# Batch 0's short rows first, the combining product in high and low halves, and new planning numbers

## The chip, the cores and the metric

The kernel runs on one core of one Trainium2 chip. The metric is device microseconds of one execution, the median of several runs. TensorE (PE) multiplies into PSUM; VectorE (DVE), ScalarE (ACT) and GpSimd (POOL) do the elementwise work; SyncE (SP) issues most of the loads and stores.

## The reference

Four batches of channel attention, whose result goes straight into a gated convolution. Cut to what is computed, with B = 4, N = 6336 rows, C = 256 channels, K = 5 taps:

```python
qn = q / (norm(q, axis=1) + 1e-06);  kn = k / (norm(k, axis=1) + 1e-06)
a = softmax(kn.transpose(0, 2, 1) @ qn / tau)        # 256 x 256 for each batch
x = v @ a
gate = sigmoid(sum(conv_w[j] * xp[:, j:j + S, :] for j in range(K)))  # xp: x with 4 zero rows ahead
out = (gate * (x @ w_val)) @ w_out
```

The three weights (`w_val`, `conv_w`, `w_out`) arrive as float64; q, k and v as float32.

## The kernel before, in words

**Scores.** N is 49 times 128 rows and 64 more, the *short rows* (`RP` = 49, `REST` = 64). For each batch the products k^T q are summed over the rows in one PSUM bank, `s_ps`. Row sets of 128 are loaded in groups of three (`GROUP`), the first group of a batch holding one. A row set is multiplied either whole in fp32 (`raw`; two products, one for each half of the channels) or split: ACT casts it to a high half `hi` (fp32r), POOL makes the low half `lo`, and PE does hi·hi, lo·hi and hi·lo, six products of 256 columns. In batch 0 two or three row sets of each group are done whole, in the first groups of batch 1 two. `group_tasks` (line 387 on) makes these tasks: `L` the load (line 402), `C` and `O` the halves, `S` the square on ACT (line 453) and `A` its addition to `acc_ps` on DVE or to `acc` on POOL (line 457), `P` the products (line 485). In batches 1 to 3 the short rows come with the first group, behind its full row set; in batch 0 they are a group of their own, put in at place 9 (`REST_AT`). Before the first data are there, PE multiplies zeros: eleven products (`idle(11)`), and four more after the first row set (`idle(4)`).

**Softmax.** Once a batch's rows are summed, `softmax_tasks` runs a chain over all engines: the sums of squares are joined (line 545), `norms` brings them onto the partitions by PE (line 535), then root, inverse, scale, exponentials (line 579), their sum, and the division (line 591) to the attention `a`. It is cast to halves (line 595 high, POOL low), which are the weights of the *mixing product* x = v·a. Further on, PE transposes `a` (line 604), ACT copies the transpose from PSUM to `at` (line 608), and the *combining product* `combine` multiplies it with w_val (line 614): four fp32 products of 256 columns, which give a·w_val, the weights of the *value product* v·(a·w_val). Its halves are made by `high_w` on ACT (line 618) and `low_w` on DVE (line 621).

**Output steps.** Thirteen steps of up to 508 positions for each batch, 52 in all. v comes in transposed (line 682) and is split (lines 686, 689). A step has two mixing products `X`, one for each half of the channels (six fp32r products each, into one of two buffers of `x_ps`), the first tap by ACT (`G`, line 720), the other taps by DVE (`D`, line 723: eight in a step), the sigmoid, two value products `U` (into `val_ps`), their multiplication with the gate on DVE (`B`, line 741), the split of the result (lines 747, 750), four output products with w_out (`F`, line 769), copies by ACT (line 778) and the store. The output products of a step stand behind the value products of the next one in PE's order.

**PSUM.** `s_ps` and `acc_ps` have a bank each, `x_ps` two, and the other four banks (tag `bank`) are shared by `val_ps`, `o_ps` (norms, transposes, combining and output products) and `w_ps` (below).

**Weights.** The float64 words are turned into float32 on DVE in ten or eleven steps of one instruction (`prepare_weights`, lines 317 to 349), spread among its other work; `WORDS` is 2 here. w_out ends as a high and a low half (`wo_hi`, `wo_lo`), w_val as one fp32 array in `wa`.

**What sets the order.** Two things. `line` (lines 861 to 909) is PE's order, written as a loop: the row groups are spread over the output steps, at such a pace that the last of them falls into step `LAST_ROWS` = 52 - 13 - `LATE`, and behind a batch's last group come its `norms`, `transpose` and `combine`, each some places apart (`SPREAD`). Steps behind LAST_ROWS give the last tap of their second half to ACT and POOL (`shared`, line 806), and every other one of those two or more further on puts `x_ps` in the banks of `s_ps` and `acc_ps` (`late`). The class `Plan` then walks through all tasks with a cost for each (`deadlines`, `run`): on each engine it takes the one that is due first by `line`, by the chain behind it, and by `WANTED` (latest wanted times for the weights). The order so found is what each engine runs; `NARROW`, `REACH` and the costs written in each `task` call feed it. So a change of one number can move instructions on all engines.

## Time and profile before

| | |
|---|---|
| median of the runs | 595.4 us (three runs, 595.34 to 595.72) |
| the profiled execution | 594.63 us |
| its span | 592.8 us |
| TensorE clock granted | 1.00 |
| DMA, mean over the span | 179 GB/s |
| score products, line 485, lo·hi and hi·lo | 306 each, 285 and 283 ns |
| mixing and value products, line 697 | 416 each, 385 and 380 ns |

The span runs from the first to the last instruction that the profiler records; the execution's own time is 1.8 us longer, and is what the runs measure. PE's matmuls are pipelined, so the mean time of one matmul is longer than the distance from its start to the next one's; where the text compares costs on PE it uses distances between starts. A matmul in unsplit fp32 leaves two records in the profile, one in fp32r leaves one. Views name a tile by its program's name and an instruction by the line that issued it.

### The profile page before, as it was taken

How to read it: one execution, taken by the hardware profiler on the slowest of the kernel's cores; microseconds unless marked ns; L12 is line 12 of the kernel's file. 1: busy time of each engine (PE TensorE's matmuls, PEld its weight loads, DVE VectorE, ACT ScalarE, POOL GpSimd, SP SyncE). 2: the span in 40 equal slices, each digit the busy share in tenths (PEclk: the TensorE clock that was granted, in tenths of full speed). 3: DMA queues.
4: the chain of work that ended last, by engine and by line, in shares of the span. 5: the costliest groups of instructions: out<-in, count | busy, mean ns of one | idle time of the engine just before them, and what ended most of it. 6: DMA issues, size and time to landing. Idle time of an engine off the chain costs nothing.

```text
span 592.8 us, 10519 instructions
## 1 busy us (share of the span) xinstructions
PE 587.0 (99%) x3647; PEld 531.8 (90%) x3647; DVE 507.5 (86%) x783; ACT 476.6 (80%) x580; POOL 511.7 (86%) x247
## 2 busy tenths in 40 slices
PE   9999999999999999999999999999999999999997
PEld 8998888989989989989988898998998898888887
DVE  3998899999998989969879898978978988888784
ACT  6787998889899878778789987878767877777754
POOL 5996999999989999999997999999993868777843
PEclk9999999999999999999999999999999999999999
DMA  8999959775659978779555897869845265554214
GB/s 343 367 379 293 256 125 196 186 188 132 173 142 217 209 181 208 143 202 223 146 153 155 209 205 201 163 145 237 157 111 118 73 142 133 133 142 121 70 41 123
DMA packets 154944, 105.83 MB, mean 179 GB/s; under 512 B 111115, under 2 KB 137995, under 8 KB 154891
## 3 DMA queue, kind: packets, MB, share of 16 engines
q1 hardware_dynamic: 154467, 104.51, 69.8%
q8 instruction: 29, 0.48, 0.3%
q10 hardware_dynamic: 423, 0.65, 0.3%
q14 instruction: 25, 0.20, 0.1%
HBM read 79.18 MB, written 25.95 MB: 177 GB/s over the span
## 4 chain that ended last, share of the span: by engine, by line
PE 93%; ACT 3%; DVE 2%; issue 1%; POOL 0%; ACTq 0%; DVEq 0%; POOLq 0%
PE s_ps L485 25%; PE o_ps L769 22%; PE x_ps L697 22%; PE val_ps L697 22%; DVE gate L723 1%; PE o_ps L614 1%; ACT hi L426 0%; ACT sq L453 0%; ACT gate L734 0%; ACT o_sb L778 0%; DVE o_ps L564 0%; PE o_ps L535 0%; ACT gate L720 0%; PE x_ps L769 0%; ACT L553 0%
## 5 line engine op out<-in xcount | busy, mean ns | idle before, releaser
L723 DVE SCALAR_TENSOR_TENSOR gate<-x_ps,wa,gate 128x508 f32<-128x508 f32 (+1 forms) x401 | 267.6, 716 | 22.9 <-ACT gate L720 21.1
L429 POOL TENSOR_TENSOR lo<-raw,hi 128x1536 fp32r<-128x1536 f32 (+2 forms) x65 | 182.4, 2811 | 12.1 <-ACT hi L426 10.7
L689 POOL TENSOR_TENSOR v_lo<-v_raw,v_hi 128x1024 fp32r<-128x1024 f32 (+1 forms) x52 | 123.4, 2375 | 12.5 <-ACT v_hi L686 12.5
L750 POOL TENSOR_TENSOR g_lo<-gate,g_hi 128x1016 fp32r<-128x1016 f32 (+2 forms) x52 | 120.4, 2316 | 15.9 <-ACT g_hi L747 15.7
L457 DVE TENSOR_TENSOR acc_ps<-acc_ps,sq 128x512 f32<-128x512 f32 (+1 forms) x139 | 96.4, 694 | 33.8 <-ACT sq L453 30.5
L697 PE MATMUL x_ps<-v_hi,w 128*128 128x512 f32 (+2 forms) x416 | 110.2, 385 | 0.3 <-DVE gate L723 0.3
L697 PE MATMUL val_ps<-v_hi,w 128*128 128x508 f32 (+1 forms) x416 | 107.6, 380 | 0.0
L453 ACT ACTIVATE sq<-raw 128x1536 f32<-128x1536 f32 (+2 forms) x68 | 96.1, 1415 | 4.6 <-DMA raw<-in_k_dram 2.1
L426 ACT CAST hi<-raw 128x1536 fp32r<-128x1536 f32 (+2 forms) x65 | 77.8, 1204 | 15.8 <-DMA raw<-in_k_dram 11.9
L697 PEld LDWEIGHTS val_ps<-v_hi,w 128*128 128x128 f32 x416 | 75.9, 188 | 14.8
L778 ACT COPY o_sb<-o_ps 127x512 f32<-127x512 f32 (+1 forms) x99 | 57.5, 587 | 35.5 <-PE o_ps L769 35.3
L697 PEld LDWEIGHTS x_ps<-v_hi,w 128*128 128x128 f32 x416 | 73.2, 188 | 13.6 <-PE o_ps L769 0.5
L769 PE MATMUL o_ps<-wo_hi,g_hi 128*127 128x256 f32 (+1 forms) x396 | 80.0, 283 | 0.6 <-ACT o_sb L778 0.6
L769 PE MATMUL o_ps<-wo_lo,g_hi 128*127 128x256 f32 (+1 forms) x396 | 78.9, 281 | 0.0
L457 POOL TENSOR_TENSOR acc<-acc,sq 128x512 f32<-128x512 f32 (+1 forms) x53 | 68.8, 1298 | 9.7 <-ACT acc L448 6.4
L485 PE MATMUL s_ps<-lo,hi 128*128 128x256 f32 x306 | 76.7, 285 | 0.0
L485 PE MATMUL s_ps<-hi,lo 128*128 128x256 f32 x306 | 76.1, 283 | 0.0
L720 ACT ACTIVATE gate<-x_ps,wa 128x508 f32<-128x508 f32 (+1 forms) x104 | 67.4, 663 | 5.9 <-PE x_ps L697 5.4
L741 DVE TENSOR_TENSOR gate<-val_ps,gate 128x508 f32<-128x508 f32 (+1 forms) x104 | 66.7, 653 | 5.8 <-PE val_ps L697 3.0
L686 ACT CAST v_hi<-v_raw 128x1024 fp32r<-128x1024 f32 (+1 forms) x52 | 57.6, 1108 | 16.2 <-PE val_ps L697 12.9
L769 PEld LDWEIGHTS o_ps<-wo_hi,g_hi 128*127 128x127 f32 (+1 forms) x396 | 62.9, 187 | 3.9 <-ACT o_sb L778 0.8
L747 ACT CAST g_hi<-gate 128x1016 fp32r<-128x1016 f32 (+3 forms) x54 | 53.0, 981 | 16.2 <-DVE gate L741 15.5
(89 smaller groups left out, 946.3 us busy)
## 6 DMA issues: line engine op xcount, KB each, us to landing
raw<-in_q_dram SPq DMA_DIRECT2D x64, 384.0 KB, 5.9
v_raw<-in_v_dram SPq DMA_DIRECT2D x192, 128.0 KB, 6.1
raw<-in_k_dram SPq DMA_DIRECT2D x63, 384.0 KB, 6.6
out_dram<-o_sb SPq DMA_DIRECT2D x47, 448.0 KB, 3.2
out_dram<-o_sb SPq DMA_DIRECT2D x47, 60.0 KB, 3.0
v_raw<-in_v_dram SPq DMA_DIRECT2D x16, 64.0 KB, 2.4
out_dram<-o_sb SPq DMA_DIRECT2D x3, 240.0 KB, 2.6
raw<-in_q_dram SPq DMA_DIRECT2D x4, 128.0 KB, 3.1
```

Of the source, the lines that this page charges most:

```text
L426: nc.scalar.copy(t["hi"][r, js], t["raw"][r, js, :, :])
L429: nc.gpsimd.tensor_tensor(t["lo"][r, js], t["raw"][r, js, :, :], t["hi"][r, js].bitcast(F32), ALU.subtract)
L453: nc.scalar.activation(t["sq"][0:np_, ja:jb], t["raw"][0:np_, ja:jb], AF.Square)
L457: eng.tensor_tensor(st[key][0:np_], st[key][0:np_], t["sq"][0:np_, j], ALU.add)
L485: nc.tensor.matmul(st["s"][:, h, :], lhs, rhs, start="open" not in st, stop=stop)
L689: nc.gpsimd.tensor_tensor(t["vl"][:, :, 0:g, :], t["v"], t["vh"][:, :, 0:g, :].bitcast(F32), ALU.subtract)
L697: nc.tensor.matmul(dst, weights[b][:, which, ws, ch, hs], vs[:, ch, at + lo:at + hi_], start=n_ == 0, stop=n_ == len(ops) - 1)
L720: nc.scalar.activation(t["gate"][:, h, 0:w], t["x", h][:, 0:w], AF.Copy, scale=cw[:, h, 0:1])
L723: nc.vector.scalar_tensor_tensor(t["gate"][:, h, 0:w], t["x", h][:, k_:k_ + w], cw[:, h, k_:k_ + 1], t["gate"][:, h, 0:w], ALU.mult, ALU.add)
L741: nc.vector.tensor_tensor(t["gate"][:, h, 0:w], t["val", h][:, 0:w], t["gate"][:, h, 0:w], ALU.mult)
L750: eng.tensor_tensor(t["gl"][:, hs, 0:w], t["gate"][:, hs, 0:w], t["gh"][:, hs, 0:w].bitcast(F32), ALU.subtract)
L769: nc.tensor.matmul(t["o", p][0:rows, u * C:(u + 1) * C], gs[:, h, j * rows:(j + 1) * rows], ws[:, h, :], start=(u, n_) == (0, 0) if HEADS ...
```

## The change

Four things are done.

**Short rows.** In every batch the short rows now belong to the first group, and in batch 0 they stand ahead of its one full row set, in the loads, on PE, and in the squares. Batch 0's group of its own is gone, as is `REST_AT`. The zeros are nine at first, and none after the first row set.

**Combining product.** w_val is kept as two fp32r halves, `wv_hi` and `wv_lo`, as w_out was. Its preparation on DVE has one step less (the halves are not added), and ACT casts the high half (`high_weights`, line 356). The transposed attention is kept as halves too: ACT's copy rounds to `at_hi`, and a new DVE task `low_at` (line 610) makes `at_lo`. `combine` then has twelve fp32r products (hi·hi for all four blocks, then at_hi·wv_lo, then at_lo·wv_hi) in place of four fp32 ones.

**Planning numbers.** `SPREAD` has an entry for each batch, `LATE` is 5 (LAST_ROWS 34, not 35), `NARROW` is a set of batches with the same one in it, `REACH` and four times in `WANTED` differ, and the costs of the changed tasks are new.

**Order.** With these the plan comes out anew on all engines; of the 192 additions of squares DVE does 144 and POOL 48, where it was 139 and 53. PE's last 607 products are the same as before.

```diff
-START, HOP, DRAIN, SLOT, FLIGHT, REACH, RATE = 3.7, 0.12, 0.22, 0.45, 4.5, 1.5, 340000.0
+START, HOP, DRAIN, SLOT, FLIGHT, REACH, RATE = 3.7, 0.12, 0.22, 0.45, 4.5, 1.6, 340000.0
...
-NARROW, LATE = 1, 4
-SPREAD = ((0, 2, 2), (0, 1, 1, 1))
-REST_AT = 9
+NARROW, LATE = (0,), 5
+SPREAD = ((0, 0, 0, 0), (1, 2, 1), (1, 2, 2), (0, 1, 1))
 TABLE = 1.28
-WANTED = {("load", "conv"): 30, ("load", "val"): 17, ("load", "out"): 40, ("ready", "val"): 40, ("ready", "conv"): 36, ("ready", "out"): 60}
+WANTED = {("load", "conv"): 26, ("load", "val"): 17, ("load", "out"): 36, ("ready", "val"): 40, ("ready", "conv"): 34, ("ready", "out"): 66}
...
-    groups = {b: [(j, n, bool(b and REST and not j)) for j, n in rows_] for b in range(B)}
-    if REST:
-        groups[0].insert(REST_AT, (0, 0, True))
+    groups = {b: [(j, n, REST > 0 and not j) for j, n in rows_] for b in range(B)}
...
-    wv_sb = wa[:, 0:NW].rearrange("p (h e) -> p h e", h=NH)
...
+    halves_w = {part: [const.tile([P, NH, C], F32R, name=f"w{part[0]}_{side}") for side in ("hi", "lo")] for part in ("val", "out")}
+    (wv_hi, wv_lo), (wo_hi, wo_lo) = halves_w["val"], halves_w["out"]
...
-            if part != "out":
+            if part == "conv":
                 yield
                 nc.vector.tensor_tensor(w, w, fs, ALU.add)
...
+    def high_weights(part):
+        if WORDS == 2:
+            nc.scalar.copy(flat(halves_w[part][0]), w_high[part])
+
+    PREP = {"val": 10, "conv": 11, "out": 10}
...
-        parts = [(P, 0, n)] * (n > 0) + [(REST, n, 1)] * rest
+        parts = [(P, 0, n)] + [(REST, n, 1)] * rest
+        if b == 0:
+            parts.reverse()
...
+            for np_, j, nj in parts:
+                for s, src in ((0, q), (1, k)):
+                    rows = src[b, 0:RP * P].rearrange("(p j) c -> p j c", j=RP)[:, j0_:j0_ + n, :] if np_ == P else src[b, RP * P:N].unsqueeze(1)
+                    (nc.scalar if apart and s else nc.sync).dma_start(out=raw[0:np_, s, j:j + nj, :], in_=rows)
...
-                idle(11)
+                idle(9)
...
-            if (b, g, j) == (0, 0, 0):
-                idle(4)
...
-            nc.scalar.copy(t["at"].rearrange("p h c -> p (h c)"), t["at_ps"])
+            t["at"] = [soft_p.tile([P, NH, C], F32R, name=f"at_{side}") for side in ("hi", "lo")]
+            nc.scalar.copy(flat(t["at"][0]), t["at_ps"])
+
+        def low_at():
+            nc.vector.tensor_tensor(flat(t["at"][1]), t["at_ps"], flat(t["at"][0]).bitcast(F32), ALU.subtract)
 
         def combine():
             t["aw"] = ps.tile([P, 512], F32, name="o_ps", tag="bank")
-            for h in range(NH):
-                for h2 in range(NH):
-                    nc.tensor.matmul(t["aw"][:, h * C:(h + 1) * C], t["at"][:, h2, h * P:(h + 1) * P], wv_sb[:, h2, :],
-                                     start=h2 == 0, stop=h2 == NH - 1)
+            ops = [(x, y, h, h2) for x, y in ((0, 0), (0, 1), (1, 0)) for h in range(NH) for h2 in range(NH)]
+            for x, y, h, h2 in ops:
+                nc.tensor.matmul(t["aw"][:, h * C:(h + 1) * C], t["at"][x][:, h2, h * P:(h + 1) * P], halves_w["val"][y][:, h2, :],
+                                 start=(x, y, h, h2) == ops[0], stop=(x, y, h, h2) == ops[-1])
...
-        task(k_("combine"), "PE", 1.65, combine, deps=[k_("copy_at"), ("ready", "val"), ("prep", "val", PREP["val"] - 1 if WORDS == 2 else 0)], uses=[aw_i], takes=[aw_i])
+        task(k_("low_at"), "DVE", 0.6, low_at, deps=[k_("copy_at")], uses=[at_i])
+        task(k_("combine"), "PE", 1.4, combine, deps=[k_("copy_at"), k_("low_at"), ("ready", "val")], uses=[aw_i], takes=[aw_i], lead={k_("low_at"): 0.9})
...
-            for key, wait in zip(names, SPREAD[b < NARROW] if b else (0,) * 4):
+            for key, wait in zip(names, SPREAD[b]):
```

Rows of the queues, in the order in which each engine runs them, show where the instructions went; a row has the line, the operation, the written tile and the ones read, its size, and how often it repeats. PE's first products, before:

```order
L485 MATMUL s_ps<-zeros 128x256 x11
L485 MATMUL s_ps<-raw 128x256 x2
L485 MATMUL s_ps<-zeros 128x256 x4
L485 MATMUL s_ps<-raw 128x256 x16
L485 MATMUL s_ps<-hi 128x256 x2
```

and of the change:

```order
L486 MATMUL s_ps<-zeros 128x256 x9
L486 MATMUL s_ps<-raw 128x256 x20
L486 MATMUL s_ps<-hi 128x256 x2
L486 MATMUL s_ps<-lo,hi 128x256
L486 MATMUL s_ps<-hi,lo 128x256
```

The first two of the twenty whole products are the short rows', the next two the first full row set's; six products of zeros are gone.

PE at the first output step: the last score products ahead of it, value products `val_ps` of step 0 and mixing products `x_ps` of step 1. Before:

```order
L485 MATMUL s_ps<-lo,hi 128x256
L485 MATMUL s_ps<-hi,lo 128x256
L697 MATMUL val_ps<-v_hi,w 128x508 x4
L697 MATMUL val_ps<-v_lo,w 128x508 x2
L697 MATMUL x_ps<-v_hi,w 128x512 x4
L697 MATMUL x_ps<-v_lo,w 128x512 x2
L697 MATMUL x_ps<-v_hi,w 128x512 x4
L697 MATMUL x_ps<-v_lo,w 128x512 x2
L697 MATMUL val_ps<-v_hi,w 128x508 x4
L697 MATMUL val_ps<-v_lo,w 128x508 x2
```

and of the change:

```order
L486 MATMUL s_ps<-lo,hi 128x256
L486 MATMUL s_ps<-hi,lo 128x256
L486 MATMUL s_ps<-hi 128x256 x8
L700 MATMUL x_ps<-v_hi,w 128x512 x4
L700 MATMUL x_ps<-v_lo,w 128x512 x2
L700 MATMUL x_ps<-v_hi,w 128x512 x4
L700 MATMUL x_ps<-v_lo,w 128x512 x2
L700 MATMUL val_ps<-v_hi,w 128x508 x4
L700 MATMUL val_ps<-v_lo,w 128x508 x2
L700 MATMUL val_ps<-v_hi,w 128x508 x4
L700 MATMUL val_ps<-v_lo,w 128x508 x2
```

The first value product of step 0 stood ahead of the mixing products of step 1; now both value products stand behind them, and eight score products of high halves ahead.

ACT at batch 0's combining product, from the copy of the transposed attention to the first taps of step 0 (`gate`). Before:

```order
L608 COPY at<-o_ps 128x512
L595 CAST w<-a 128x512
L376 CAST wo_hi<-w_ps 128x512
L686 CAST v_hi<-v_raw 128x1024
L426 CAST hi<-raw 128x512
L618 CAST w<-o_ps 128x512
L720 ACTIVATE gate<-x_ps,wa 128x508 x2
```

and of the change:

```order
L607 CAST at_hi<-o_ps 128x512
L594 CAST w<-a 128x512
L356 CAST wo_hi<-w_ps 128x512
L454 ACTIVATE sq<-raw 128x1536
L689 CAST v_hi<-v_raw 128x1024
L427 CAST hi<-raw 128x512
L723 ACTIVATE gate<-x_ps,wa 128x508
L620 CAST w<-o_ps 128x512
L723 ACTIVATE gate<-x_ps,wa 128x508
```

A square of three row sets has come in behind the cast of w_out, and the high half of the combined weights (`w<-o_ps`) stands between the two first taps.

More of the change, by code (lines that the diff above doesn't have):

```diff
@@ L286 @@
     NW = NH * C
-    wa = const.tile([P, NW + NH * K], F32, name="wa")
-    wb = const.tile([P, NW], F32, name="wb")
-    wv_sb = wa[:, 0:NW].rearrange("p (h e) -> p h e", h=NH)
-    cw = wa[:, NW:].rearrange("p (h k) -> p h k", h=NH)
-    wo_hi = const.tile([P, NH, C], F32R, name="wo_hi")
-    wo_lo = const.tile([P, NH, C], F32R, name="wo_lo")
-    parts_w = {"val": wa[:, 0:NW], "conv": wa[:, NW:], "out": wb}
+    w_conv = const.tile([P, NH * K], F32, name="wa")
+    cw = w_conv.rearrange("p (h k) -> p h k", h=NH)
+    halves_w = {part: [const.tile([P, NH, C], F32R, name=f"w{part[0]}_{side}") for side in ("hi", "lo")] for part in ("val", "out")}
+    (wv_hi, wv_lo), (wo_hi, wo_lo) = halves_w["val"], halves_w["out"]
+    flat = lambda w: w.rearrange("p h e -> p (h e)")
+    parts_w = {"conv": w_conv}
+    for part in ("val", "out"):
+        parts_w[part] = flat(halves_w[part][1]) if WORDS == 2 else const.tile([P, NW], F32, name=f"w{part[0]}_sb")
     w_raw, w_high = {}, {}
@@ L339, in prepare_weights @@
             yield
-            low = wo_lo.rearrange("p h e -> p (h e)") if part == "out" else w
-            nc.vector.scalar_tensor_tensor(low, lo, 2.0 ** -35, fs, ALU.mult, ALU.mult)
+            nc.vector.scalar_tensor_tensor(w, lo, 2.0 ** -35, fs, ALU.mult, ALU.mult)
             yield
@@ L348, in prepare_weights @@
             w_high[part] = fs
-            if part != "out":
+            if part == "conv":
                 yield
                 nc.vector.tensor_tensor(w, w, fs, ALU.add)
-        elif part == "out":
-            nc.vector.tensor_copy(wo_hi, wb.rearrange("p (h e) -> p h e", h=NH))
-            nc.vector.tensor_tensor(wo_lo, wb.rearrange("p (h e) -> p h e", h=NH), wo_hi.bitcast(F32), ALU.subtract)
-    PREP = {"val": 11, "conv": 11, "out": 10}
+        elif part != "conv":
+            hi, low = map(flat, halves_w[part])
+            nc.vector.tensor_copy(hi, w)
+            nc.vector.tensor_tensor(low, w, hi.bitcast(F32), ALU.subtract)
+    def high_weights(part):
+        if WORDS == 2:
+            nc.scalar.copy(flat(halves_w[part][0]), w_high[part])
+    PREP = {"val": 10, "conv": 11, "out": 10}
     def weight_tasks():
@@ L373, in weight_tasks @@
                      uses=[holds[part], ("bank", "w", part)], takes=[("bank", "w", part)] if k == 0 else [])
-            task(("ready", part), "DVE" if part == "conv" else "ACT" if part == "out" else None, 0.5 if part == "out" else 0.07,
-                 {"val": lambda: None, "conv": lambda: nc.vector.reciprocal(rtau, tau_sb),
-                  "out": lambda: WORDS == 2 and nc.scalar.copy(wo_hi.rearrange("p h e -> p (h e)"), w_high["out"])}[part],
+            task(("ready", part), "DVE" if part == "conv" else "ACT", 0.07 if part == "conv" else 0.5,
+                 (lambda: nc.vector.reciprocal(rtau, tau_sb)) if part == "conv" else lambda part=part: high_weights(part),
                  deps=[("prep", part, n - 1)], uses=[holds[part], ("bank", "w", part)])
@@ L402, in load @@
             raw = raw_p.tile([P, 2, GROUP, C], F32, name="raw")
-            for s, src in ((0, q), (1, k)):
-                if n:
-                    main = src[b, 0:RP * P].rearrange("(p j) c -> p j c", j=RP)
-                    (nc.scalar if apart and s else nc.sync).dma_start(out=raw[:, s, 0:n, :], in_=main[:, j0_:j0_ + n, :])
-                if rest:
-                    nc.sync.dma_start(out=raw[0:REST, s, n, :], in_=src[b, RP * P:N])
+            for np_, j, nj in parts:
+                for s, src in ((0, q), (1, k)):
+                    rows = src[b, 0:RP * P].rearrange("(p j) c -> p j c", j=RP)[:, j0_:j0_ + n, :] if np_ == P else src[b, RP * P:N].unsqueeze(1)
+                    (nc.scalar if apart and s else nc.sync).dma_start(out=raw[0:np_, s, j:j + nj, :], in_=rows)
             if (b, g) == (0, 1):
@@ L413, in group_tasks @@
         apart = b == 0 and g < 2
-        task(("L", b, g), "SP", ((n * P + REST * rest) * C * 8, 1 if apart else 2 * ((n > 0) + rest), 1), load, takes=[raw_i], uses=[raw_i])
+        task(("L", b, g), "SP", ((n * P + REST * rest) * C * 8, (1 if apart else 2) * (1 + rest), 1), load, takes=[raw_i], uses=[raw_i])
         if g == 0:
```

9 lines of the change are left out of this document (4 added, 5 removed).

## The prediction

> **What bounds the kernel.** I read the page first: the span, the busy shares, and the chain of work that ended last. Then the waits of TensorE (PE), longest first in total: engine, line, what it waited for, microseconds in total, times, longest.
>
> ```profile
> span 592.8 us, 10519 instructions
> ...
> PE 587.0 (99%) x3647; PEld 531.8 (90%) x3647; DVE 507.5 (86%) x783; ACT 476.6 (80%) x580; POOL 511.7 (86%) x247
> ...
> PE 93%; ACT 3%; DVE 2%; issue 1%; POOL 0%; ACTq 0%; DVEq 0%; POOLq 0%
> ```
> ```profile
> PE s_ps L485 <- DVE zeros L277: 1.2, 1, 1.2
> PE o_ps L769 <- ACT o_sb L778: 0.6, 1, 0.6
> PE x_ps L697 <- DVE gate L723: 0.3, 1, 0.3
> PE o_ps L614 <- ACT at L608: 0.2, 1, 0.2
> ```
>
> PE is busy for 99% of the span, 93% of the chain is PE, and its waits add up to 2.3 us. So the time is the sum of PE's products, their waits, and a fixed head and tail. An edit gains what it takes off PE's queue and loses what it makes PE wait; the other engines count only where they make PE wait. How close they are to that is seen in the busy times by stage (stretch, its length, then busy time and count of each engine):
>
> ```profile
> 60.00:200.00 140.00, 140.00 (x885) 126.74 (x884) 132.12 (x200) 127.08 (x147) 135.26 (x57) 1.00 0.76 181
> ```
>
> In this first stage with output work, DVE is busy for 132 of 140 us, ACT for 127 and POOL for 135. Little is left there for a helper that falls behind.
>
> **The change, part by part.**
>
> *The start.* PE's first instructions in order of time (start, length, line, operands, count):
>
> ```profile
> 1.19 2.71 PE L485 MATMUL s_ps<-zeros 128*128 128x256 f32 x11 [1.19 <-DVE zeros L277]
> 3.70 1.97 PE L485 MATMUL s_ps<-raw 128*128 128x256 f32 x4
> 5.11 1.22 PE L485 MATMUL s_ps<-zeros 128*128 128x256 f32 x4
> 6.17 7.07 PE L485 MATMUL s_ps<-raw 128*128 128x256 f32 x32
> ...
> 23.58 1.89 PE L485 MATMUL s_ps<-raw 128*128 128x256 f32 x8
> 25.12 0.59 PE L485 MATMUL s_ps<-hi 128*128 128x256 f32 x2
> ...
> 26.12 3.07 PE L485 MATMUL s_ps<-raw 64*128 64x256 f32 x12
> 28.83 0.59 PE L485 MATMUL s_ps<-hi 128*128 128x256 f32 x2
> ```
> ```profile
> 3.57 0.60 ACT L448 ACTIVATE acc_ps<-raw 128x512 f32<-128x512 f32 x1 [0.41 <-DMA raw<-in_k_dram]
> 5.81 1.06 ACT L453 ACTIVATE sq<-raw 128x1024 f32<-128x1024 f32 x1 [1.64 <-DMA raw<-in_k_dram]
> ```
>
> An unsplit fp32 product leaves two records, so the short rows are four of the twelve at 26.12. A usual stretch of eight takes 25.12 - 23.58 = 1.54 us; this one takes 28.83 - 26.12 = 2.71. Taking the short rows out of it saves **1.17 us**. They now come after nine products of zeros; the other six are gone. What does that cost at the start? Group 1 begins at 6.17 now, and its load had landed by 5.81. In its place PE does nine zeros, from 1.19 to about 3.3, then the four records of the short rows, then the four of group 0. If the short rows land where the first load lands now (3.57), their four records take the place of the four from 3.70 to 5.11 (1.41 us, at a slow rate), and group 0's four the place of the zeros behind: at 0.22 (32 records in 7.07 us) to 0.35 (1.41/4) each they end between 6.0 and 6.5. I take 6.5. Group 1's load stands 128 KB further back in the queue; even half a microsecond later, at 6.3, it is covered. So group 1 starts 0.3 later, and the start is worth 0.3 - 1.17 = **-0.85**. No row shows how soon a 64 KB load lands when nothing is queued ahead of it. The row of such loads, queued behind others (count, size, median us from issue to landing), is
>
> ```profile
> raw<-in_q_dram SPq DMA_DIRECT2D x4, 64.0 KB, 4.9
> ```
>
> The bounds: if they land before the zeros end at 3.3, nothing is lost and the term is -1.17; if they take 4.9 us, they land near 5.6, PE idles for two microseconds, and the term is about +0.8. I take the value next to the first load's.
>
> The rows of batch 0 then end 0.85 earlier. Does the softmax start earlier too?
>
> ```profile
> 45.00 0.69 DVE L545 TENSOR_TENSOR acc_all<-acc_ps,acc 128x512 f32<-128x512 f32 x1
> ...
> 47.88 0.97 PE L535 MATMUL o_ps<-ones,acc_all 128*128 128x1 f32 x8
> ```
>
> The sums of squares are ready at 45.7 and PE asks for them at 47.88: a cover of 2.2 us. DVE gets one addition and one weight step more before that sum, 1.3 us; the early addition of the short rows falls into its idle start. The cover stays, if only by a few tenths.
>
> *The combining product.* Batch 1's, with the output products behind it, and two of the split products of rows:
>
> ```profile
> 176.67 0.28 PE L485 MATMUL s_ps<-lo,hi 128*128 128x256 f32 x1
> 176.79 0.28 PE L485 MATMUL s_ps<-hi,lo 128*128 128x256 f32 x1
> ...
> 183.33 1.89 PE L614 MATMUL o_ps<-wa,at 128*128 128x256 f32 x8
> 184.87 0.58 PE L769 MATMUL o_ps<-wo_hi,g_hi 128*127 128x256 f32 x2
> 185.29 0.40 PE L769 MATMUL o_ps<-wo_lo,g_hi 128*127 128x256 f32 x2
> ```
>
> It holds PE for 184.87 - 183.33 = 1.54, and the pair behind it takes 0.42 where two cost 0.24: 1.72 in all. Split products of 256 columns follow each other at 0.12; twelve take 1.44. That is 0.28 less for each of batches 1 to 3, and 0.4 for batch 0, which shows 1.65 + 0.19: **-1.25**. The last four need the low half, which DVE makes. Behind batch 1's transposes PE has some 5.8 us of other products, and seven taps of 0.7 (5.58/8, a row below) stand ahead of the low half on DVE; behind batch 3's it has 2.8 us, against three taps; in batch 0 the eight products ahead (0.96) cover DVE's 0.69 (such a pass as the sum above). I count no wait for it, and if a cover is gone, each tap too many costs its 0.7.
>
> The Trainium skill (FP8 and Floating Point Precision, TensorE Precision Notes) has a true fp32 product as four passes through the array, and (TensorE: Matmul & The Clock Gate, Back-to-back issue gap) a pass of N columns as N/2.4 + 2.5 ns, 109 ns here; by this estimate 12 passes in place of 16 would save 0.44 us a batch, and the sum below would be -2.4. The trace agrees on four passes (1.72 us for four products) but has 120 ns for a single pass with its own weights, so the row stands.
>
> *Queues ordered anew, at the first output step.* In the new order PE does the row products, eight more of the next groups, and both mixing products of step 1 ahead of any value product. The second mixing product needs a buffer that DVE's eight taps of step 0 must have read. ACT's path to those taps, then DVE and PE:
>
> ```profile
> 51.78 1.47 ACT L453 ACTIVATE sq<-raw 128x1536 f32<-128x1536 f32 x1
> 53.17 0.51 ACT L579 ACTIVATE s<-s,m 128x256 f32<-128x256 f32 x1
> ...
> 57.90 0.58 ACT L608 COPY at<-o_ps 128x512 f32<-128x512 f32 x1 [1.19 <-PE o_ps L604]
> ...
> 59.37 1.16 ACT L686 CAST v_hi<-v_raw 128x1024 fp32r<-128x1024 f32 x1
> 60.41 0.65 ACT L426 CAST hi<-raw 128x512 fp32r<-128x512 f32 x1
> 60.93 0.61 ACT L618 CAST w<-o_ps 128x512 fp32r<-128x512 f32 x1
> 61.93 0.68 ACT L720 ACTIVATE gate<-x_ps,wa 128x508 f32<-128x508 f32 x1 [0.39 <-PE x_ps L697]
> ```
> ```profile
> 62.65 5.58 DVE L723 SCALAR_TENSOR_TENSOR gate<-x_ps,wa,gate 128x508 f32<-128x508 f32 x8 [0.38 <-ACT gate L720]
> ```
> ```profile
> 58.53 1.99 PE L614 MATMUL o_ps<-wa,at 128*128 128x256 f32 x8 [0.19 <-ACT at L608]
> 60.18 0.81 PE L697 MATMUL x_ps<-v_hi,w 128*128 128x508 f32 x2
> ...
> 63.11 1.89 PE L485 MATMUL s_ps<-raw 128*128 128x256 f32 x8
> ...
> 65.55 1.09 PE L697 MATMUL val_ps<-v_hi,w 128*128 128x508 f32 x4
> ...
> 66.94 1.15 PE L697 MATMUL x_ps<-v_hi,w 128*128 128x512 f32 x4
> ...
> 68.38 1.17 PE L697 MATMUL x_ps<-v_hi,w 128*128 128x512 f32 x4
> ```
>
> Let t be the start of the copy after the transposes, 57.90 now. The first gate starts at t + 4.03, and from there to the second mixing product it is 68.38 - 61.93 = 6.45. In the new order a square of 1.39 (53.17 - 51.78) stands between: 1.47 to the square, 1.39, 1.04 and 0.52 give t + 4.42, so the buffer is free at t + 10.87. PE gets there at 0.63 + 1.44 (combining) + 2.74 (first mixing products, 2.93 less the 0.19 above) + 2.44 (row products) + 0.96 (eight at 0.12) + 1.44 = t + 9.65. It waits for 1.2 us; some 0.1 of waiting that stands there today goes: **+1.1**. Without the square's delay it would be 0.7; if the next casts are late too, 2.
>
> *The old waits.* The wait of 0.6 is for a free PSUM bank behind batch 2's combining product, the one of 0.3 for taps behind batch 3's transposes. In the new order the first comes later behind more products, and the second uses the banks that the score sums have left (LATE is 5, not 4). I let both go: **-0.9**, from 0 (kept) to -1.2 (with the gaps around them).
>
> *At nothing:* the taps and additions that move between DVE, ACT and POOL (PE's products cover them outside the first step), the loads' new order (no wait of PE in the list above names a load; if one came to, it would cost what it lands late), the tail, whose last 607 products are the same.
>
> Sum: -0.85 - 1.25 + 1.1 - 0.9 = **-1.9**. The profiled execution took 594.63 with a span of 592.8, so it would take 592.7 with 590.9. The runs' median, 595.4, is 0.8 above the profiled one: 595.4 - 1.9 = **593.5**.
>
> **Rivals.** (a) *The waits stay*: both old waits are only moved and the first step's wait is 1.5. For it: DVE and POOL at 94% and 97% in the stage shown. Against it: only four waits before. 593.5 + 0.9 + 0.4 = 594.8. (b) *The short rows don't replace the zeros*: their loads land late, PE idles (term +0.8): 593.5 + 1.65 = 595.1. For it: today's first load lands at 3.57, hardly ahead of the product of it at 3.70. Against it: 64 KB are half of that load. (c) *The clock*: eleven zeros take 0.23 each where split products take 0.12 later; the fast rate begins between 5.11 and 6.17, some 4.4 us after the first product. Should the gap at 3.3 start this stretch again, 4.4 us would hold 2.2 us of work: 595.7. The Trainium skill (TensorE: Matmul & The Clock Gate, What's actually happening) has half rate until about 3.4 us of sustained work, in windows that run free; by that a gap of 0.2 changes little. (d) *Slower: DVE bounds the first steps.* Today the second mixing product of step 1 starts at 68.38, 0.2 after the taps end (62.65 + 5.58): there is no margin. If DVE, with its extra additions and low halves, stays as late in steps 1 to 3 as in step 0, each costs another 1.3: 593.5 + 3.9 = 597.4. It decides from the point where DVE's work for a step exceeds PE's. Against it: over the stage of 140 us DVE is busy for 132, so it catches up once a late start is past.
>
> **How the numbers follow.** Forecast 0.55 (its own range 592.3 to 594.3), (a) 0.20, (b) 0.07, (c) 0.05, (d) 0.13. About 0.2%, 1.2 us, is what a measurement can tell from no change, so faster is under 594.2, slower over 596.6. Faster: 0.53 of the forecast and 0.05 of (a); same: the rest of these with (b) and (c); slower: (d) and a trace of (a). The best ends of all terms come to 591.8; 596.0 takes in (a), (b) and (c), and (d) is left out.
>
> **What would show it.** After: twelve combining products at 0.12 with no wait before the ninth; the raw products of group 1 at 6.2 to 6.6; the first product of norms at about 47.0; a wait of about 1.2 before step 1's second mixing product; no wait above 0.4 later. It is wrong if PE idles near 3 us, if the norms wait for the sums, or if waits for taps go on past step 1.

## The result, and the profile after

The changed kernel takes **598.81 us** (median of 8 runs, 597.30 to 600.91); the kernel before, beside it, 595.19 (8 runs, 594.26 to 595.86). The ratio is **1.0061, 95% interval 1.0043 to 1.0080**: slower by 3.6 us, where 1.9 us faster was forecast, and outside the range. The runs also spread over 3.6 us, more than twice as far as before.

The page of the changed kernel, its span, busy times and the chain by engine:

```profile
span 595.2 us, 10532 instructions
...
PE 587.9 (99%) x3657; PEld 531.6 (89%) x3657; DVE 515.2 (87%) x790; ACT 474.4 (80%) x582; POOL 507.1 (85%) x243
...
PE 92%; DMA 3%; ACT 2%; issue 0%; SPq 0%; POOL 0%; DVE 0%; ACTq 0%; POOLq 0%
...
```

PE is still the bound, and the chain has a new entry: 3% of it is DMA, where none was. It begins with a load, and three more loads stand further on (start, length, what):

```profile
0.74 2.90 DMA raw<-in_q_dram
3.78 44.56 PE s_ps L486 x226
...
51.55 4.42 DMA raw<-in_k_dram
...
58.19 6.25 DMA raw<-in_q_dram
...
317.29 7.09 DMA raw<-in_k_dram
```

Before, the chain began with PE's zeros, which covered the first load; now PE waits for one. The last of the loads further on leads, by way of ACT, to the wait of 1.1 below (at 327.01). At the other two ACT had no idle time, so nothing is read from them. PE's waits in that profile (what, for whom, us in total, times, longest):

```profile
PE s_ps L486 <- DVE zeros L274: 1.2, 1, 1.2
PE o_ps L772 <- ACT o_sb L781: 1.1, 1, 1.1
PE s_ps L486 <- ACT hi L427: 0.4, 1, 0.4
PE s_ps L486 <- DMA raw<-in_q_dram: 0.3, 1, 0.3
PE o_ps L534 <- ACT o_sb L781: 0.3, 1, 0.3
```

The wait for a bank was to go, and has grown from 0.6 to 1.1. Ahead of the copy that ends it, ACT casts a high half. Before, and then in the change:

```profile
329.91 1.47 ACT L426 CAST hi<-raw 128x1536 fp32r<-128x1536 f32 x1
331.29 0.57 ACT L778 COPY o_sb<-o_ps 127x512 f32<-127x512 f32 x1
```
```profile
324.48 1.48 ACT L427 CAST hi<-raw 128x1536 fp32r<-128x1536 f32 x1 [1.84 <-DMA raw<-in_k_dram]
...
326.38 0.58 ACT L781 COPY o_sb<-o_ps 127x512 f32<-127x512 f32 x1
```

Before, ACT had no idle time ahead of that cast; in the change it sat idle for 1.84 us until the load of k landed, which the chain shows at 317.29 with 7.09 us.

The waits explain only part: the other part is PE running slowly, which no list of waits shows. It is in the start. PE's first high products come 2.4 us later. Before, and then in the change, with the row that holds all whole products ahead of them:

```profile
12.89 0.59 PE L485 MATMUL s_ps<-hi 128*128 128x256 f32 x2
```
```profile
3.78 11.87 PE L486 MATMUL s_ps<-raw 64*128 64x256 f32 x40 [0.30 <-DMA raw<-in_q_dram]
15.30 0.59 PE L486 MATMUL s_ps<-hi 128*128 128x256 f32 x2
```

The profile in stretches of time (stretch, length, then busy time and count of PE, PEld, DVE, ACT, POOL; clock, DMA share, GB/s), before:

```profile
2.00:4.00 2.00, 2.00 (x10) 2.00 (x10) 0.00 (x0) 1.58 (x3) 0.00 (x0) 1.00 0.94 322
...
8.00:9.00 1.00, 1.00 (x7) 0.90 (x6) 0.00 (x0) 1.00 (x1) 0.76 (x1) 1.00 1.03 415
```

and after:

```profile
2.00:4.00 2.00, 1.70 (x8) 1.44 (x8) 0.00 (x0) 1.49 (x2) 0.00 (x0) 1.00 0.79 195
...
8.00:9.00 1.00, 1.00 (x4) 0.73 (x4) 0.00 (x0) 1.00 (x2) 0.00 (x0) 1.00 1.01 399
```

Two things are other than before. From 2 to 4 us the DMA engines move 195 GB/s in place of 322, though they are busy for 0.79 of the time (0.94 before). And from 8 to 9 us, when both kernels do whole products of 128 rows without a wait, PE gets through 4 records in place of 7 (a whole product leaves two). They follow each other at 0.43 us, which is called the half rate here, against 0.22 later. It lasts to 9.5 us, where it had ended at 5.9. Yet the busy share is 1.00 in both, and so is the clock column: only the count shows it.

SyncE's queue and ACT's first work show the loads. SyncE issuing the first loads of q, before:

```profile
0.74 1.35 SPq L406 DMA_DIRECT2D raw<-in_q_dram  x3
```

and after, with ACT's first squares of group 0 and of group 1, each released by a landing:

```profile
0.74 2.41 SPq L409 DMA_DIRECT2D raw<-in_q_dram  x4
```
```profile
5.79 0.60 ACT L449 ACTIVATE acc_ps<-raw 128x512 f32<-128x512 f32 x1 [1.85 <-DMA raw<-in_q_dram]
...
7.42 0.63 ACT L449 ACTIVATE acc<-raw 128x512 f32<-128x512 f32 x1 [0.49 <-DMA raw<-in_q_dram]
```

An issue takes 0.60 us on the average of its row, where it took 0.45. Group 0 is there at 5.79 (3.57 before) and group 1 at 7.42 (5.81). But PE does not wait for group 1: the list of waits has one wait for a load, 0.3 us for the short rows' own, in the row at 3.78. By the starts of its records PE gets to group 1 at 7.67 (6.17 before), since the four records of the short rows take 2.03 us and the four of group 0 another 1.86. From there to the first high product it takes 7.63, where it took 6.72. So in this profile the slow products are nearly all of the 2.4 us, and the late landing of group 1 is hidden behind them.

**Where the time went, by stage.** From each profile I add up the distances between the starts of PE's products and take off a fixed price for each (0.216 us a record of a whole product, 0.120 a split one, 0.2285 a mixing or value product, 0.118 an output product, nothing for zeros and combining products). What is left is time that PE lost, by waits, slow products, zeros and combining:

| profile (its time) | batch 0's rows | its softmax, first steps | batch 1 | batch 2 | batch 3, end |
|---|---|---|---|---|---|
| before (594.63) | 4.85 | 2.41 | 2.78 | 3.65 | 2.69 |
| before, again (596.86) | 5.46 | 2.38 | 3.35 | 4.51 | 2.97 |
| after (597.32) | 6.00 | 3.08 | 2.79 | 4.05 | 2.81 |
| after, again (596.66) | 6.35 | 3.09 | 2.26 | 4.02 | 2.40 |

The combining products, at 0.3 us less in each batch, are in these numbers; so the stages behind the start, which should have gained 1.3 and the old waits besides, gained nothing.

### The profile page after: what moved, and what is told of

The parts are those of the page before. It is cut to its first block, busy times and chain, and to the rows that moved or that the text cites. A ratio compares the mean times of both kernels' runs of the same rounds, so it can differ in the third digit from the quotient of the medians.

```text
span 595.2 us, 10532 instructions
## 1 busy us (share of the span) xinstructions
PE 587.9 (99%) x3657; PEld 531.6 (89%) x3657; DVE 515.2 (87%) x790; ACT 474.4 (80%) x582; POOL 507.1 (85%) x243
## 4 chain that ended last, share of the span: by engine, by line
PE 92%; DMA 3%; ACT 2%; issue 0%; SPq 0%; POOL 0%; DVE 0%; ACTq 0%; POOLq 0%
PE s_ps L486 24%; PE o_ps L772 23%; PE val_ps L700 22%; PE x_ps L700 22%; DMA raw<-in_k_dram 2%; DMA raw<-in_q_dram 2%; ACT hi L427 1%; PE o_ps L616 0%; ACT v_hi L689 0%; ACT sq L454 0%; PE o_ps L536 0%; ACT o_sb L781 0%; PE x_ps L772 0%; ACT gate L723 0%; PE o_ps L534 0%
## 5 line engine op out<-in xcount | busy, mean ns | idle before, releaser
L726 DVE SCALAR_TENSOR_TENSOR gate<-x_ps,wa,gate 128x508 f32<-128x508 f32 (+1 forms) x400 | 272.6, 717 | 33.2 <-ACT gate L723 28.9
L458 DVE TENSOR_TENSOR acc_ps<-acc_ps,sq 128x512 f32<-128x512 f32 (+1 forms) x144 | 99.8, 693 | 24.9 <-ACT sq L454 21.4
L458 POOL TENSOR_TENSOR acc<-acc,sq 128x512 f32<-128x512 f32 (+1 forms) x48 | 62.6, 1304 | 10.5 <-ACT sq L454 8.7
L737 ACT ACTIVATE gate<-gate 128x1016 f32<-128x1016 f32 (+1 forms) x52 | 53.2, 1023 | 18.6 <-DVE gate L726 18.5
```

The costliest lines, as they stand in the source:

```text
L458: eng.tensor_tensor(st[key][0:np_], st[key][0:np_], t["sq"][0:np_, j], ALU.add)
L726: nc.vector.scalar_tensor_tensor(t["gate"][:, h, 0:w], t["x", h][:, k_:k_ + w], cw[:, h, k_:k_ + 1], t["gate"][:, h, 0:w], ALU.mult, ALU.add)
```

## The experiments

Each was timed beside the kernel before on the same chip; "over before" is the difference of the two medians. A name in a diff such as ("S", 1, 3, 0) is a task: kind, batch, group, part. The diffs show only the lines that tell the edits apart. Where an order is kept, the plan's order was taken as it came out, and only the named tasks moved in it (`place` puts the first task right ahead of the second).

| run | median, us (lowest to highest) | over before | ratio, 95% |
|---|---|---|---|
| again (the change) | 599.03 (596.66 to 602.22) | +3.7 | 1.0043 to 1.0092 |
| zeros13 | 598.26 (597.12 to 598.61) | +2.9 | 1.0033 to 1.0061 |
| row_first | 599.82 (596.51 to 602.67) | +4.4 | 1.0047 to 1.0098 |
| row_first_z11 | 598.95 (597.90 to 600.57) | +3.6 | 1.0051 to 1.0086 |
| start_back | 602.36 (602.13 to 602.60) | +7.0 | 1.0107 to 1.0134 |
| tables_back | 601.30 (598.80 to 604.26) | +5.9 | 1.0100 to 1.0139 |
| start_tables_back | 602.02 (599.78 to 603.50) | +6.6 | 1.0095 to 1.0131 |
| before_again | 595.43 (594.35 to 596.86) | 0.0 | 0.9991 to 1.0008 |
| halves_only | 595.94 (595.07 to 599.14) | +0.7 | 0.9998 to 1.0025 |
| start_only_back | 595.80 (594.45 to 597.52) | +0.6 | 0.9993 to 1.0015 |
| square_later | 599.59 (598.03 to 602.24) | +4.4 | 1.0048 to 1.0091 |
| start_square | 598.12 (596.71 to 598.68) | +2.9 | 1.0026 to 1.0052 |
| loads_first | 598.14 (597.45 to 601.57) | +2.4 | 1.0031 to 1.0067 |
| low_zeros | 599.28 (598.01 to 600.30) | +3.6 | 1.0045 to 1.0071 |
| value_first | 596.52 (595.19 to 600.44) | +0.8 | 1.0004 to 1.0036 |

### The start: gap, or late loads?

`again` is the change itself. `zeros13` closes the gap ahead of the first product; `row_first` puts the full row set ahead of the short rows; `row_first_z11` does that without a gap.

```diff
 # zeros13
-                idle(9)
+                idle(13)
 # row_first
-        if b == 0:
-            parts.reverse()
 # row_first_z11: both of row_first, and
-                idle(9)
+                idle(11)
```

> The changed kernel once more, for its scatter (597.3 to 600.9 so far) and a second profile of its start. Clock theory (C): TensorE reaches its fast rate only after an unbroken stretch of products; the idle gap near 3.3 us starts that stretch again, at a place that varies, so the fast rate (9.4 us in the first profile, 5.4 in the kernel before) comes at another time here, and the first product of a high half (15.30 so far) moves by half of that difference. Data theory (D): the late landing of the first loads alone sets the start; the fast rate may move, the first high product stays within 0.3 of 15.3 unless the landings move. Either way a span of 595 to 599.

> Thirteen products of zeros in place of nine, so that PE has no gap before the short rows land (3.76); all else as in the change. C: fast rate from about 5.4 us, group 1 starts when its load lands (7.4), PE waits some 0.5 for it, and the first high product comes at about 14.4 in place of 15.3: 0.9 us faster than the change. D: the loads are as late as before, the first high product stays at 15.3 or later by what the zeros hold up (0.2): no gain.

> The first full row set is loaded, multiplied and squared ahead of the short rows; nine zeros still, so that a gap of about 0.3 us is left between the zeros (end 3.3) and the first product (3.6). C: the gap still starts the slow stretch again, group 1 and part of group 2 run at half rate as in the change, the first high product comes at 14.8 to 15.3. D: the first load lands at 3.6 again and group 1 near 6.2, so the first high product comes at 13.3 to 13.6: 1.7 to 2 us faster than the change.

> As the last, with eleven zeros as in the kernel before, so that no gap is left. C and D both: fast rate from about 5.4 and group 1 near 6.2 to 6.6; the first high product at 13.2 to 13.5, 2 us faster than the change. The difference from the last run is the gap's alone: 1.5 to 2 us by C, 0.1 by D.

The gap is not it. In `zeros13` PE has no wait there that its list shows, and it is as slow; its stretches:

```profile
7.00:8.00 1.00, 1.00 (x4) 0.82 (x3) 0.00 (x0) 0.47 (x1) 0.00 (x0) 1.00 0.99 393
8.00:9.00 1.00, 1.00 (x4) 0.73 (x4) 0.00 (x0) 1.00 (x2) 0.00 (x0) 1.00 1.05 421
```

The half rate lasts to 9.5 us with the gap (10.3 in `again`) and to 9.6 without. The other order does not mend it either: in `row_first` the first row set is there at 3.6 again, but group 1 lands at 8.7 and PE idles. In `row_first_z11` the rate was full at 4.3, before the short products, and PE then idled for 1.6 us for group 1 and fell back to half rate until 11.1. So the late landing of group 1 is there in either order; PE waits for it where the full row set comes first. Something other than the gap keeps the rate low when short products come first. My expectation of 2 us gained by loading the row first was wrong.

### Taking parts back through the plan

```diff
 # start_back: the groups, zeros and loads of before; start_tables_back: this and the next
-    groups = {b: [(j, n, REST > 0 and not j) for j, n in rows_] for b in range(B)}
+    groups = {b: [(j, n, bool(b and REST and not j)) for j, n in rows_] for b in range(B)}
+    if REST:
+        groups[0].insert(9, (0, 0, True))
 # tables_back: REACH and WANTED of before too
-NARROW, LATE = (0,), 5
-SPREAD = ((0, 0, 0, 0), (1, 2, 1), (1, 2, 2), (0, 1, 1))
+NARROW, LATE = (0,), 4
+SPREAD = ((0, 0, 0, 0), (0, 2, 2), (0, 2, 2), (0, 2, 2))
```

> The start of the kernel before (short rows as a group at place 9, eleven and four products of zeros) with the rest of the change. The loads of group 1 are issued at 1.2 us again and land near 5.7 (7.4 in the change), the first high product comes at 12.9 in place of 15.3, and with the short rows' 1.2 us later the time is 1.1 to 1.2 below the change's in profiles: a span of 594.0. Theory S: the change's scatter (596.5 to 602.2) comes from when its first loads land; here the runs lie within 2 us, with a median near 596.3. Rival: the scatter comes from the middle of the program; the runs still spread over 4 us and the median is 597.7.

> The change with the planning numbers of before (SPREAD (0, 2, 2) for batches 1 to 3, LATE 4, REACH, WANTED). Theory T: the waits that PE has in the change from 150 us on (2.8 us: for a free bank ahead of norms and output products, near 165, 326, 419 and 455) come with the numbers; here they are back to the 1.4 of before, the first step's 1.1 stays (the order there is the same), and the time is 1.4 below the change's. Rival: they come with the combining product in halves, whose low half and casts load DVE and ACT; they stay at 2.5 to 3 and the time is within 0.5 of the change's.

> The combining product in halves alone, start and numbers as before. By the sum of the stages: -1.3 for the four combining products, +1.1 for the first step, whose products stand in the new order here too, and the old waits: 595.2. If the first step's wait is not there, 594.1. By the rival of the last run (waits come with the halves) 596.5.

> The kernel before, for a second profile of its start and its own spread: 594.3 to 596.5, a fast rate from between 4.2 and 6.5 us with the time following by at most half of that, group 1's loads landing at 5.5 to 6.0.

Three misses, and all slower than the change, by 2 to 3.5 us. The starts did as told (`start_back` loses 5.17 in batch 0's rows), but every one of these edits makes the plan come out anew on all engines, and PE then lost up to 6 us in a later stage (`start_back`: 6.13 in batch 1, 5.78 in batch 2; `tables_back`: 5.33 in batch 3), above all waiting for POOL's low halves and DVE's taps. These runs do not tell the parts apart, since they compare whole plans. What they do show is that the change's planning numbers belong to its own plan. From here on the order was kept.

### One part at a time, in a kept order

```diff
 # start_only_back: the change, but the start
+            if (b, g) == (0, 9):
+                state[0]["short"] = short = const.tile([P, 2, 1, C], F32, name="short")
+                for s, src in ((0, q), (1, k)):
+                    nc.sync.dma_start(out=short[0:REST, s, 0, :], in_=src[0, RP * P:N])
+        for key, x in ((("P", 0, 0, 1), "P"), (("S", 0, 0, 0), "S"), (("A", 0, 0, 1), "A")):
+            place(order, key, (x, 0, 9, 0))
-                idle(9)
+                idle(11)
+            if (b, g, j) == (0, 0, 0):
+                idle(4)
 # square_later: the change, but a square of ACT and its additions; start_square: both
+        place(order, ("S", 1, 3, 0), ("C", 1, 6, 0))
+        for j, x in ((0, ("M", 0, "low_w")), (2, ("M", 0, "low_w")), (1, ("O", 1, 6, 0))):
+            place(order, ("A", 1, 3, j), x)
 # halves_only: the kernel before, with combine in halves and low_at put into its order
+            start = next(x[0] for x in order if x[1] == ("M", b, "copy_at")) + 0.6
```

> The change with every instruction in its own order, but for the start, which is that of the kernel before: short rows loaded into a tile of their own just ahead of group 9, multiplied, squared and added there; eleven and four products of zeros. P: group 1's load lands near 5.6 again, the first high product comes at 12.9, the stages behind are as in the change: 1.1 to 1.2 less, a span of 594 in the profile, and a spread of the runs of 2 us or less, median 596.5. Q: the earlier start runs into waits that are as long; the later stages lose 0.5 to 1.2 more than in the change, median 598 or more.

> The kernel before with every instruction in its old order, and only the combining product in halves: w_val's high half cast where its preparation ends, the low half of the transposed attention put on DVE 0.6 us (by the plan's clock) behind ACT's copy. Theory P (the change's loss lies in its start and its order, not in the halves): 1.3 us less on PE, no new wait over 0.3: a median of 594.1. Rival Q (DVE and ACT have no room for the added passes): new waits of 1 us or more between 150 and 460 us, median 595 to 597.

> The change with one square of ACT (1.5 us, ahead of the first gate of step 0) moved behind both gates and the next cast, and its additions on DVE behind the eight taps; nothing else moves. P: the first gate starts 1.4 us earlier, the taps end at about 68.4, the waits of PE between 66 and 68 us (1.1 in all) go, and the second mixing product of step 1 starts at 68.7 in place of 69.9: 1.1 less. If only the gates mattered and the casts stay late, 0.6 less; if the additions behind the taps hold up the low half of the combined weights, the first value product waits for 0.5.

> Both of the last two. P: 2.2 to 2.3 less than the change, a span of 592.9 in the profile and a median of 595.3, what is left over the kernel before being the waits from 150 us on, against the halves' gain. Q: less than 1.2 in all.

**The start is nearly all of the loss.** With the start of before and everything else of the change, the kernel is 0.6 us over before, not clear of nothing, where the change is 3.6 to 3.7 over. So the start costs some 3 us. Group 1 is there in time again; ACT's first square of it:

```profile
5.78 0.63 ACT L453 ACTIVATE acc<-raw 128x512 f32<-128x512 f32 x1 [1.36 <-DMA raw<-in_q_dram]
```

**The halves gain nothing.** `halves_only` should have been 1.3 us faster and is 0.7 over before. On PE the products do what was worked out. In the change, batch 1's combining product and the value product behind it:

```profile
182.75 0.63 PE L616 MATMUL o_ps<-wv_hi,at_hi 128*128 128x256 f32 x4
183.22 0.63 PE L616 MATMUL o_ps<-wv_lo,at_hi 128*128 128x256 f32 x4
183.69 0.63 PE L616 MATMUL o_ps<-wv_hi,at_lo 128*128 128x256 f32 x4
184.15 1.07 PE L700 MATMUL val_ps<-v_hi,w 128*128 128x508 f32 x4
```

184.15 - 182.75 = 1.40, with no wait before the ninth, where four fp32 products cost 1.72. But in `halves_only`, with the old order, the output product behind batch 2's combining product waits longer for the same copy. First before, then `halves_only`:

```profile
331.91 0.51 PE L769 MATMUL o_ps<-wo_hi,g_hi 128*127 128x256 f32 x2 [0.62 <-ACT o_sb L778]
```
```profile
332.90 0.50 PE L777 MATMUL o_ps<-wo_hi,g_hi 128*127 128x256 f32 x2 [0.98 <-ACT o_sb L786]
```

0.62 has become 0.98: PE comes 0.3 us earlier and waits that much longer, since ACT sets the time. In batch 3 PE waits twice for taps (0.30 and 0.40) where it waited once (0.31). By the stages, `halves_only` keeps 0.3 of its gain at batch 0 (2.08 lost there, 2.41 before) and 0.1 in batch 1 (2.65, 2.78), and none in batches 2 and 3 (4.23 and 2.93, where before shows 3.65 and 2.69 in one profile and 4.51 and 2.97 in the other). The medians say the same: no gain.

**square_later** was wrong outright: `start_square`, which has the same edit, is 2.3 us slower than `start_only_back`. ACT's queue in `square_later`, and PE's longest wait there:

```profile
60.99 1.11 ACT L689 CAST v_hi<-v_raw 128x1024 fp32r<-128x1024 f32 x1 [0.91 <-DVE v_raw L685]
```
```profile
PE s_ps L486 <- ACT hi L427: 1.7, 1, 1.7
```

Where the square had been, ACT now waits 0.91 us for DVE's transpose: the square had stood in a hole. The gates come only 0.4 earlier, and the square now delays the next cast, for which PE waits 1.7.

### What in the start costs it

```diff
 # loads_first: start_only_back, but the short rows' loads first of all, k's on ACT
-            if (b, g) == (0, 9):
+            if (b, g) == (0, 0):
 # low_zeros: start_only_back, but products of zeros of 64 rows
-                product(zeros[:, 0:P], zeros, 0)
+                product(zeros[0:64, 0:P], zeros[0:64], 0)
 # value_first: start_only_back, and
+        place(order, ("U", 0, 0), ("P", 1, 5, 0, "hi"))
+        place(order, ("M", 0, "low_w"), ("D", 0, 0, 2))
```

> start_only_back (median 595.8) with one thing changed: the two 64 KB loads of the short rows are issued first of all, as in the change, though their products still stand ahead of group 9. Loads theory: group 1's loads are issued 1 us later and land at 6.5 to 8.7 (5.4 to 5.8 in start_only_back); PE idles 1 to 3 us ahead of group 1, whose products may run at half rate again; the median rises by 1.5 to 3 and the runs spread over 3 us or more. Clock theory (the short rows' products at the front keep the clock low, the loads do no harm): within 0.5 of start_only_back.

> start_only_back with one thing changed: the fifteen products of zeros use 64 rows of the array in place of 128, as the short rows' products do. Clock theory: products of 64 rows don't count as work for the clock, so the half rate, which ended between 4.5 and 7.5 us in the six profiles with the old start, ends at 8 to 11, counted from the full products at 5.9; group 1 runs at half rate and the median rises by 1 to 1.5. Loads theory, or height of no matter: half rate ends between 4.5 and 7.5, the median stays within 0.5 of 595.8.

> start_only_back with one edit at the first output step: the first value product of step 0 stands ahead of the eight high products and of step 1's mixing products again, and the low half of its weights on DVE behind the first tap. Theory: what PE lost there (1.1 us, first at the cast of the high products, and had that been on time at the taps) is covered by the 1.4 us of the value product, but for what the low half puts on the taps (0.7): 0.6 to 0.8 less, median 595.1. Rival: the loss moves to step 2's mixing products, for whose buffer DVE had 0.4 us to spare: within 0.3 of start_only_back.

**Both hurt, each without the other's edit.** `loads_first` has the early loads, not the early products: 2.4 over before in place of 0.6. PE's first row set and group 1, and two stretches:

```profile
4.70 2.07 PE L491 MATMUL s_ps<-raw 128*128 128x256 f32 x4 [0.79 <-DMA raw<-in_q_dram]
...
8.03 6.15 PE L491 MATMUL s_ps<-raw 128*128 128x256 f32 x25 [0.40 <-DMA raw<-in_q_dram]
```
```profile
2.00:4.00 2.00, 1.90 (x9) 1.61 (x8) 0.00 (x0) 1.49 (x2) 0.00 (x0) 1.00 0.91 216
...
8.00:9.00 1.00, 0.97 (x2) 0.84 (x3) 0.00 (x0) 1.00 (x2) 0.00 (x0) 1.00 1.03 402
```

PE waits for both, and the rate is 216 GB/s again. The half rate lasts to about 9.0 us here, though every product is of full height; so the 1.8 us over `start_only_back` are not the two waits of 0.79 and 0.40 alone. `low_zeros` has every load in time, no early short row, and only the zeros' products lower: 3.6 over before. Its stretches, and below them one of `start_only_back`:

```profile
8.00:9.00 1.00, 1.00 (x4) 0.82 (x3) 0.00 (x0) 1.00 (x1) 0.56 (x1) 1.00 1.05 421
9.00:10.00 1.00, 1.00 (x4) 0.82 (x3) 0.86 (x2) 0.53 (x2) 0.78 (x1) 1.00 1.03 406
```
```profile
8.00:9.00 1.00, 1.00 (x6) 0.91 (x5) 0.09 (x1) 1.00 (x1) 0.71 (x1) 1.00 1.03 415
```

The half rate lasts to 9.9 us. In the eight profiles with full-height zeros and the old start it ended between 4.6 and 7.5; in the eight that have the change's start or `zeros13`'s, at 8.2 to 10.3. Zeros of 64 rows do not bring the full rate. That the short rows' products, of 64 rows too, do the same in the change is argued from this and from the eight profiles; no run has the short rows first at full height. The single effects (1.8 and 3.0 over `start_only_back`) add up to more than the change's 3. The traces of the change show why they need not add up: in none of its five profiles does PE's list show a wait for group 1, which at the half rate it reaches only after the landing.

**value_first** gains nothing over `start_only_back` in the runs, and 0.2 in the stage in question (2.91 lost, 3.09). The loss has moved to the second mixing product of step 2 (at 77.38), as the rival in its expectation had it:

```profile
PE x_ps L708 <- DVE gate L734: 0.5, 1, 0.5
```

### Three more profiles of the change

> The change once more, one profiled execution, to catch one of its slower ones. If the executions above 598.5 lose their time at the start, such a profile has group 1's loads landing at 8 us or later and PE's half rate lasting to 10.5 or later (7.4 and 9.4 in the first profile, 7.3 and 10.4 in the second), and the time of the stages behind batch 0's rows within 1 us of the 12.7 and 11.8 lost there so far. If they lose it later, the start looks as in the first two and the stages behind lose 2 us more.

> The change once more, one profiled execution. A slow one (over 598.5) has its loss at the start (loads of group 1 at 8 us or later, half rate to 10.5 or later), or else 2 us more of it behind batch 0's rows; a fast one looks as the first two profiles.

> The change once more, one profiled execution. A slow one (over 598.5) has its loss at the start (loads of group 1 at 8 us or later, half rate to 10.5 or later), or else 2 us more of it behind batch 0's rows; a fast one looks as the first two profiles.

They are single executions, beside one of the kernel before of 595.65. They took 595.49, 595.95 and 597.86: none lies above 598. The first two lose 5.31 in batch 0's rows, with the half rate to 8.5 and 8.2; the third 6.22, to 10.3, and 4.76 in batch 2. So the five profiled executions of the change have a mean of 596.7, 2 us under the median of its timed runs, and lose 5.8 on the mean in batch 0's rows, where the eight profiles with the old start lose 4.6 to 5.8, 5.2 on the mean. Of the 3 us, the profiles thus show the slow start but only a part of the size. What the executions above 598 do is in no profile; that it hangs on the start is shown by `start_only_back`, whose one difference removes it.

## Why the prediction was wrong, point by point

- **The start, -0.85: the step that failed.** It stood on two sentences. "At 0.22 to 0.35 each" was the distance of the first products, and this is what cost the time. They ran at 0.43, and the half rate went on for 3.6 us longer. The 0.35 was the 1.41 us of the first row set divided by four; but by the starts of its records the distances are 0.49, 0.43 and 0.43, and then 0.07, where the zeros follow. So 0.43 could be had from the trace of before. Group 0 was to be done by 6.5, and PE got to group 1 at 7.67. "Even half a microsecond later, at 6.3, it is covered" was the landing of group 1: it came 1.6 later in the profile, behind two more loads in the queues. It was covered nonetheless, by the slow products: PE has no wait for it. `loads_first`, whose landings are late too, does wait. The first high product came at 15.30 in place of 12.89, 2.4 late. With the 1.2 saved later the term is +1.2 between those two profiles and about +3 in the timed runs.
- **Rivals (b) and (c)** named two mechanisms that are there, late loads and a slow rate, and got 7% and 5%. (b) looked at the short rows' own landing, which cost 0.3 (products from 3.78); it is the loads behind that are late. (c) put the slow rate down to a gap; `zeros13` has no such wait and is as slow, and `low_zeros` shows that the height of the first products matters. It named 2.2 us; `low_zeros` costs 3.0.
- **A row of the Trainium skill** speaks against the change, and I did not use it: SBUF — State Buffer, Door 1: The DMA port swizzle, says that a load into partitions 0 to 63 reaches only 8 of the 16 ports and measured 196 GB/s at 1 MiB, against 328 for all 128. The trace has 195 GB/s from 2 to 4 us, against 322. That goes the same way, but it does not measure the short loads: they are 128 KB of the 390 KB or so that were moved there, and the queues were only starting.
- **The combining product, -1.25**: on PE as worked out (1.40 for 1.72, four times 0.3), with the low half in time. Wrong was to add it to the sum in full: `halves_only` shows that behind batches 2 and 3 it is given back in a wait that ACT and DVE end.
- **The first output step, +1.1**: the size was right (3.08 lost where 2.41 was, though the combining product there saves 0.3: +1.0), and so was the time at which the taps end. The wait was another. ACT's copy after the transposes in the change, and DVE's taps:

```profile
59.05 0.59 ACT L607 CAST at_hi<-o_ps 128x512 fp32r<-128x512 f32 x1 [1.19 <-PE o_ps L603]
```
```profile
64.16 5.58 DVE L726 SCALAR_TENSOR_TENSOR gate<-x_ps,wa,gate 128x508 f32<-128x508 f32 x8 [0.67 <-ACT gate L723]
```

  The taps end at 69.74, t + 10.69 (forecast 10.87). But PE had no wait there: it lost the time a little earlier, at ACT's cast of the halves for the eight high products (the wait of 0.4 in the list), and came to the second mixing product at 69.86, just behind the taps. That the square behind it could be moved away for a gain was not so.
- **The old waits, -0.9**: the one for a bank has grown (0.6 to 1.1), the one for taps has gone from the list, and a new one of 0.3 came at the norms. Rival (a) was nearer. Behind the wait of 1.1 stands a load, by the rows above: ACT sat idle for 1.84 us until it landed. The prediction had put the loads' new order at nothing, because no wait of PE named a load; but PE's list names ACT here, and only the chain and ACT's row name the load. No run moves that load or that cast alone. `start_only_back` has this wait too (1.2), so it is no part of what the start costs.
- **The range:** its lower end, 591.8, takes the first step's term as nothing, while the lowest value given for it is 0.7; with that the best ends come to 592.5.
- **Rival (d)** did not happen: the steps behind the first lose nothing (-0.1 in the change between 80 and 160 us).

Open: how late the first loads and the full rate are in the executions above 598 us. No version beat the kernel before; the nearest, `start_only_back` and `halves_only`, are within the measure of it.

## What to carry to other kernels

Work in the place of filler is free only if its data, and its load on the queue, come free too: small loads put first delay the large ones behind them, and filler may be what brings the clock up. Microseconds taken off the bound engine ahead of a wait that another engine ends are not gained; look for the next such wait before adding them to a sum. A wait that is put down to one engine may stem from a load that this engine waited for: follow the chain, not only the list. Where a planner sets the order, undo a part in a kept order: letting it plan again compares two plans, not two parts.

## What was not expected of the hardware

- Products of zeros that use 64 of the 128 rows did not raise PE's rate: full rate after 9.9 us with low zeros (`low_zeros`, one profile), after 4.6 to 7.5 with full ones (eight). The clock column of the profile shows 1.00 throughout; the distance of the products (0.43 and 0.22 us) shows it.
- The Trainium skill (TensorE: Matmul & The Clock Gate, What's actually happening) has the full rate after one busy window of 3.4 us that runs free. The eight old starts agree: 3.4 to 6.3 us from the first product at 1.19.
- Two loads of 64 partitions by 1 KB at the head of the queues cost 1.8 us of the whole time (`loads_first` against `start_only_back`).
